# Chunk 0 of an SSM plus SwiGLU kernel: parameters turned by a VectorE block transpose, two evictions split by K tile, activation transposes at other places

## The chip, the cores and the metric

The kernel runs on one core of a Trainium2 chip. The metric is the device time of one execution in microseconds. Every kernel of one round is timed on the same chip, next to runs of the kernel before. A ratio is the mean time of one kernel's fast runs over that of the other's of the same rounds, so it is not quite the ratio of the medians that are quoted. A fast run is within 1.5% of the fastest. One run of the kernel before (181.74 us, in the last round) lies 1.2% above its fastest, far from all others. The ratios of that round include it, and it makes them wide; the ranges, counts and medians quoted below leave it out.

## The reference, cut to what matters

```python
x = A_x                                   # 1 x 2048 x 512, bfloat16
xn = layernorm(x)
# A: diagonal state space model with complex state, 512 states
y = 2 * real(scan(Lam_bar, xn @ B_bar.T) @ C.T) + xn * Dskip
# B: SwiGLU with a hidden size of 1376
f = (silu(xn @ w_gate) * (xn @ w_up)) @ w_down
out = x + y + f
```

`Lam_bar`, `B_bar` and the rotation tables come from three parameter vectors of 512 values each: `Lambda_re`, `Lambda_im`, `log_dt`.

## The kernel before

The 2048 rows are worked in four chunks of 512, each of four tiles of 128 rows. Only chunk 0 matters here. Its tiles are normalised on VectorE and ScalarE, transposed on TensorE (two halves of 256 columns per tile, two 128x128 transposes per half), evicted from PSUM to `xnT` by ScalarE (tiles 0 to 2) or VectorE (tile 3), and multiplied at once with the first 7 column tiles of `w_gate`: 28 matmuls of 128 columns for each tile, called a quarter. Dummy matmuls run before this, to bring TensorE's clock up.

The parameters are loaded as 12 rows of 128 and turned on TensorE, ahead of the last transposes of tile 3:

```python
def pload(name, slot, src, **kw):
    return dma(name, prow[4 * slot:4 * slot + 4, :], src.rearrange("(a p) -> a p", p=128), ...)

def xt_tile_fine(a, h, slot=None):              # tile a, half h
    par = a == 3 and h == 1
    def tr2(e):
        if par:                                                                   # L577
            e.transpose(out=ptr[:, slot, 512:524], in_=prow[:], identity=ident[0:12, 0:12])
        for j in range(2):                                                        # L580
            ... e.transpose(out=ptr[:, slot, j*128:(j+1)*128], in_=xn_sb[...], identity=ident[:])
    ...
    if a == 3:            # VectorE evicts, and copies the parameters out of PSUM (L589)
    elif a == 0 and h == 0:   # ScalarE, one eviction per K tile (L593)
    else:                 # ScalarE, one eviction of 128x256 (L598)
# [cut]
pe_warm(9, 512, wbank); pe_warm(2, 128, wbank)          # dummy matmuls
ln_chunk0()
xt_tile_fine(0, 0, wbank); pe_warm(1, 256, ...); xt_tile_fine(0, 1); pe_warm(1, 256, ...)
for q in range(4):
    for k0, k1 in ((0,1),(1,2),(2,3),(3,4)) if q == 0 else ((0,2),(2,4)):
        for n, (i, bk) in enumerate(tiles):             # 7 column tiles
            if k0 == 0 and n == 1 and q:
                xt_tile_fine(q, 1)
            if k0 == (2 if q else 3) and n == (0, 2, 1, 9)[q]:
                xt_tile_fine(q + 1, 0)
            ... matmul w_gate tile i with xnT of quarter q, K tiles k0 to k1      # L804
```

All transposes of chunk 0 after the first share one PSUM slot, so each must also wait until the previous one is evicted.

## Time and profile before

| | before |
|---|---|
| median of 3 runs | 179.68 us (179.66 to 179.74) |
| span of the profiled execution | 177.8 us |
| TensorE's share of the chain that ended last | 95% |
| quarters of chunk 0, TensorE | 5.93 to 13.42 us |

The page of the kernel before, busy times and the chain by engine:

```profile
PE 173.9 (98%) x936; PEld 83.7 (47%) x936; DVE 163.1 (92%) x284; ACT 88.3 (50%) x114; POOL 9.2 (5%) x21
...
PE 95%; DMA 1%; ACT 1%; DVE 1%; issue 0%
```

TensorE is the chain, and VectorE's 92% is not. From 11.97 us to 175.5 us the chain has no piece but matmuls. So a change that edits none of those matmuls can gain only ahead of 13.42 us. This is the chain there, for the kernel before, in order of time (start us, length us, engine, output and line, count). L804 are the quarters' matmuls, L580 the activation transposes, L577 the parameter transpose, and L760 is the first matmul of 512 columns:

```profile
5.93 1.17 PE pb L804 x21
7.10 0.13 PE pb L580 x2
7.23 0.02 issue
7.25 0.39 ACT xnT L598
7.64 0.05 issue
7.69 0.28 PE pb L804 x2
7.97 0.11 PE pb L580 x2
8.09 0.89 PE pb L804 x16
8.98 0.11 PE pb L580 x2
9.09 0.76 PE pb L804 x12
9.85 0.11 PE pb L580 x2
9.97 0.78 PE pb L804 x14
...
11.64 0.11 PE pb L577
11.75 0.22 PE pb L580 x2
11.97 1.45 PE pb L804 x26
13.42 11.22 PE pb L760 x52
```

How to read it: divide length by count. 14 matmuls in 0.78 us and 26 in 1.45 us are 0.0557 us each; that is TensorE without a wait. 12 in 0.76 us are not: 0.67 would do, so 0.09 us was lost to a wait too short to be a piece of its own. At 7.25 the chain leaves TensorE for an eviction on ScalarE, the one outright wait. The pair after L577 takes 0.22 us where every other takes 0.11 to 0.13.

The timeline of the kernel before shows the same wait at the weight load (PEld), with its releaser; the eviction of tile 2's first half; and the small parameter transpose:

```profile
7.25 0.38 ACT L598 ACTIVATE xnT<-pb 128x256 bf16<-128x256 bf16 x1 [0.85 <-PE pb L580]
7.68 0.11 PEld L804 LDWEIGHTS pb<-xnT,wg 128*128 128x128 bf16 x2 [0.26 <-ACT xnT L598]
...
9.13 0.38 ACT L598 ACTIVATE xnT<-pb 128x256 bf16<-128x256 bf16 x1 [0.62 <-PE pb L580]
...
9.56 0.12 PEld L804 LDWEIGHTS pb<-xnT,wg 128*128 128x128 bf16 x2
...
11.57 0.18 PE L577 MATMUL pb<-ident,prow 12*128 12x12 bf16 x1
```

The timeline of the queue that issues the loads (SP), kernel before: the first parameter load, the load of `w_up` behind the three, and the first of the DMA transposes of B, which waits for all earlier loads:

```profile
3.13 0.37 SPq L401 DMA_DIRECT2D prow<-in_A_log_dt_dram  x1
...
4.18 0.41 SPq L401 DMA_DIRECT2D wu<-in_B_w_up_dram  x1
...
13.72 2.07 SPq L396 DMA_TRANSPOSE BT<-in_A_B_re_dram  x1
```

### The profile page before, as it was taken

Reading aid. Unit: us, or ns where it says so; the run is one execution under the profiler, and the core shown is the slowest. Engines: PE = TensorE matmul, PEld = TensorE weight load, DVE = VectorE, ACT = ScalarE, POOL = GpSimd, SP = SyncE. Lnnn points to the kernel's source line nnn. Section 1 sums busy time; section 2 is a strip of 40 time slices with the busy share of each in tenths; the row PEclk is TensorE's granted clock in tenths of the full one; section 3 lists DMA queues with packets and bytes.
Section 4 is the critical chain, followed back from the end, with each engine's and each line's share of the span. In section 5 each row is a group of like instructions: output and inputs, shape, how many; then the busy total and the mean of one; then the engine's idle time right before and its main releaser. Section 6 shows DMA issues by size and latency. Waiting matters only on the chain.

```text
span 177.8 us, 2427 instructions
## 1 busy us (share of the span) xinstructions
PE 173.9 (98%) x936; PEld 83.7 (47%) x936; DVE 163.1 (92%) x284; ACT 88.3 (50%) x114; POOL 9.2 (5%) x21
## 2 busy tenths in 40 slices
PE   8899999999999999999999999999999999999994
PEld 3794444444444444444444444444444444444743
DVE  2958998997999999999999999999899999999933
ACT  4669989699999674043565660000965520000000
POOL 3023300210000000300000000000000000000000
PEclk9999999999999999999999999999999999999999
DMA  5995563569540000012600000002000000001022
GB/s 162 382 331 118 120 122 118 121 147 329 148 79 0 0 0 0 0 33 85 123 0 0 0 0 4 0 29 81 8 0 4 0 0 0 0 0 49 13 88 89
DMA packets 22978, 12.37 MB, mean 70 GB/s; under 512 B 15192, under 2 KB 22968, under 8 KB 22968
## 3 DMA queue, kind: packets, MB, share of 16 engines
q1 hardware_dynamic: 22472, 11.54, 23.4%
q10 hardware_dynamic: 496, 0.69, 1.2%
q8 instruction: 7, 0.11, 0.3%
q14 instruction: 3, 0.02, 0.0%
HBM read 6.46 MB, written 2.10 MB: 48 GB/s over the span
## 4 chain that ended last, share of the span: by engine, by line
PE 95%; DMA 1%; ACT 1%; DVE 1%; issue 0%
PE pb L760 36%; PE pb L959 21%; PE pb L972 16%; PE pb L876 16%; PE pb L804 3%; PE pb L839 2%; DMA x_sb<-in_A_x_dram 1%; PE pb L849 1%; PE pb L580 1%; DVE st L528 0%; ACT xn_sb L546 0%; ACT xnT L598 0%; ACT sd L522 0%; ACT nm L543 0%; DVE x_sb L977 0%
## 5 line engine op out<-in xcount | busy, mean ns | idle before, releaser
L916 DVE TENSOR_TENSOR_SCAN rot<-sm,car,rot 128x512 bf16<-128x512 f32 x32 | 39.0, 1267 | 0.1
L959 PE MATMUL pb<-wd,hT 128*128 128x512 bf16 (+3 forms) x198 | 38.8, 355 | 0.0
L760 PE MATMUL pb<-xnT,wu 128*128 128x512 bf16 x160 | 37.3, 379 | 0.0
L760 PE MATMUL pb<-xnT,wg 128*128 128x512 bf16 x132 | 31.3, 379 | 0.0
L972 PE MATMUL pb<-W,hss 128*128 128x512 bf16 (+2 forms) x144 | 28.3, 355 | 0.0
L876 PE MATMUL pb<-xnT,BT 128*128 128x512 bf16 x128 | 28.1, 379 | 0.0
L959 PEld LDWEIGHTS pb<-wd,hT 128*128 128x128 bf16 (+1 forms) x198 | 18.5, 98 | 19.9
L772 ACT ACTIVATE sg<-pb 128x1024 bf16<-128x1024 f32 x20 | 20.2, 1025 | 9.4 <-PE pb L760 8.1
L760 PEld LDWEIGHTS pb<-xnT,wu 128*128 128x128 bf16 x160 | 15.6, 98 | 18.9 <-issue 0.2
L829 ACT ACTIVATE uf<-pb 128x1024 bf16<-128x1024 f32 x20 | 20.6, 1028 | 7.5 <-PE pb L760 6.1
L972 PEld LDWEIGHTS pb<-W,hss 128*128 128x128 bf16 x144 | 13.4, 98 | 14.3
L760 PEld LDWEIGHTS pb<-xnT,wg 128*128 128x128 bf16 x132 | 12.7, 98 | 15.7 <-issue 0.8
L876 PEld LDWEIGHTS pb<-xnT,BT 128*128 128x128 bf16 x128 | 12.5, 98 | 15.1
L883 ACT ACTIVATE u_sb<-pb 128x1024 bf16<-128x1024 f32 x16 | 16.3, 1022 | 6.0 <-PE pb L876 5.6
L977 DVE TENSOR_TENSOR x_sb<-pb,x_sb 128x512 bf16<-128x512 f32 (+2 forms) x18 | 11.1, 624 | 3.6 <-PE pb L972 3.4
L831 DVE TENSOR_TENSOR hT<-sg,uf 128x1024 bf16<-128x1024 bf16 x20 | 13.4, 682 | 0.4 <-ACT uf L829 0.4
L504 ACT ACTIVATE xn_sb<-x_sb,nmr,rstd 128x512 bf16<-128x512 bf16 x8 | 6.0, 802 | 9.2 <-DVE nmr L501 9.2
L858 ACT ACTIVATE sg<-pb 96x1024 bf16<-96x1024 f32 x2 | 2.0, 1020 | 17.1 <-PE pb L839 17.1
L907 DVE TENSOR_TENSOR rot<-u_sb,cosT 128x2048 bf16<-128x2048 bf16 x8 | 9.8, 1219 | 0.3 <-ACT u_sb L883 0.3
L907 DVE TENSOR_TENSOR rot<-rot,cosT 128x2048 bf16<-128x2048 bf16 x8 | 9.7, 1218 | 0.1
L907 DVE TENSOR_TENSOR rot<-rot,sin 128x2048 bf16<-128x2048 bf16 x8 | 9.8, 1219 | 0.0
L907 DVE TENSOR_TENSOR rot<-u_sb,sin 128x2048 bf16<-128x2048 bf16 x8 | 9.7, 1218 | 0.0
(82 smaller groups left out, 141.2 us busy)
## 6 DMA issues: line engine op xcount, KB each, us to landing
out_dram<-x_sb SPq DMA_DIRECT2D x15, 128.0 KB, 1.7
x_sb<-in_A_x_dram SPq DMA_DIRECT2D x3, 512.0 KB, 7.1
wd<-in_B_w_down_dram SPq DMA_DIRECT2D x1, 1280.0 KB, 6.4
wu<-in_B_w_up_dram SPq DMA_DIRECT2D x1, 768.0 KB, 5.0
wu<-in_B_w_up_dram SPq DMA_DIRECT2D x1, 608.0 KB, 7.2
x_sb<-in_A_x_dram SPq DMA_DIRECT2D x4, 128.0 KB, 3.5
wg<-in_B_w_gate_dram SPq DMA_DIRECT2D x1, 480.0 KB, 6.0
wg<-in_B_w_gate_dram ACTq DMA_DIRECT2D x1, 448.0 KB, 3.9
```

What stands on the lines that cost most here:

```text
L504: g.add("act", lambda e, a=a: e.activation(out=xn_sb[:, a % NXN, :], in_=x_sb[:, a, :], func=AF.Identity, scale=rstd[:, a:a + 1], bias=nmr ...
L760: inst = e.matmul(pbank[0:fs, bk, :].rearrange("p (j t) -> p j t", j=4), lhsT=w[:, kt, i * 128:i * 128 + fs], rhs=xnT[:, c % 2, :, kt, :], ...
L772: g.add("act", lambda e: e.activation(out=sg[rows, sl, 0:n, :].rearrange("p a t -> p (a t)"), in_=pair_f32(rows, bk, 512 * n), func=AF.Sil ...
L829: g.add("act", lambda e: e.activation(out=uf[rows, ul, 0:n, :].rearrange("p a t -> p (a t)"), in_=pair_f32(rows, bk, 512 * n), func=AF.Ide ...
L831: g.add("dve", lambda e: e.tensor_tensor(out=hT[rows, hb, i0:i0 + n, :], in0=sg[rows, sl, 0:n, :], in1=uf[rows, ul, 0:n, :], op=ALU.mult), ...
L876: inst = e.matmul(pbank[:, bk, :].rearrange("p (j t) -> p j t", j=4), lhsT=BT[:, ri, kt, pt * 128:(pt + 1) * 128], rhs=xnT[:, c % 2, :, kt ...
L883: g.add("act", lambda e: e.activation(out=u_sb[:, us].rearrange("p r t -> p (r t)"), in_=pair_f32(slice(0, 128), b0), func=AF.Identity), r ...
L907: tt = lambda out, a, b, op, r, w, nm: g.add("dve", lambda e: e.tensor_tensor(out=out, in0=a, in1=b, op=op), reads=r, writes=w, name="%s_% ...
L916: g.add("dve", lambda e, A0=A0, A1=A1, k=k, ri=ri, pt=pt: e.tensor_tensor_scan(out=A1[:, k, ri, :], data0=rr[:, pt:pt + 1].to_broadcast([1 ...
L959: inst = e.matmul(pbank[:, bk, 0:nc_], lhsT=hT[0:fs, hb, i, lt * 128:(lt + 1) * 128], rhs=wd[0:fs, i, c0:c0 + nc_], start=(i == 0), stop=F ...
L972: inst = e.matmul(pbank[:, bk, 0:nc_], lhsT=hss[:, hb, pt, ri, lt * 128:(lt + 1) * 128], rhs=W12[:, ri, pt, c0:c0 + nc_], start=False, sto ...
L977: g.add("dve", lambda e, bk=bk, a=a, c0=c0, nc_=nc_: e.tensor_tensor(out=x_sb[:, a, c0:c0 + nc_], in0=pbank[:, bk, 0:nc_], in1=x_sb[:, a, ...
```

## The change

The intent: take the parameter transpose off TensorE, and give each eviction time to end before TensorE needs it. VectorE's transpose is used on 32x32 blocks (the prediction says why), so the rows are loaded in another layout (16 rows of 32 values per vector, spread over 128 partitions), and one VectorE instruction turns them. Tiles 1 and 2 get their first half evicted by K tile, the quarters' matmuls start on the first K tile alone, and the transposes stand a few matmuls earlier or later.

```diff
-        praw = sb("praw", [128, 3, PT], B16)
-        prow = sb("prow", [12, 128], B16)
+        prT = sb("prT", [128, 32], B16)
+        praw = prT[:].rearrange("p (a e) -> p e a", e=8)
+        prow = sb("prow", [128, 32], B16)          # zeroed by GpSimd first
...
-  dma(name, prow[4 * slot:4 * slot + 4, :], src.rearrange("(a p) -> a p", p=128), ...)
+  dma(name, prow[slot:128:8, :], src.rearrange("(a q j) -> q a j", a=4, q=4), ...)
...
-                             ("r", 2, 0), ("n", 2, 0), ("n", 2, 1), ("b", 3, 1), ("s", 3, 0),
+                             ("r", 2, 0), ("n", 2, 0), ("n", 2, 1), ("b", 3, 1), ("s", 3, 0), ("p", 0, 0),
+                elif op == "p":
+                    last = g.add("dve", lambda e: e.transpose(out=prT[:], in_=prow[:]), ...)
...
-                if par:
-                    e.transpose(out=ptr[:, slot, 512:524], in_=prow[:], identity=ident[0:12, 0:12])
-                if par:
-                    g.add("dve", ... tensor_copy(out=praw..., in_=ptr[:, slot, 512:524]) ...)
-            elif a == 0 and h == 0:
+            elif h == 0:
                 for j in range(2):    # one eviction per K tile
...
+            place = {(0, 2, 4): (1, 0), (1, 0, 3): (1, 1), (1, 2, 2): (2, 0), (2, 0, 4): (2, 1), (2, 2, 2): (3, 0), (3, 0, 2): (3, 1)}
             for q in range(4):
-                for k0, k1 in ((0, 1), (1, 2), (2, 3), (3, 4)) if q == 0 else ((0, 2), (2, 4)):
+                for k0, k1 in (((0, 1), (1, 2), (2, 3), (3, 4)), ((0, 1), (1, 2), (2, 4)), ((0, 1), (1, 2), (2, 4)), ((0, 2), (2, 4)))[q]:
                     for n, (i, bk) in enumerate(tiles):
-                        if k0 == 0 and n == 1 and q:
-                            xt_tile_fine(q, 1)
-                        if k0 == (2 if q else 3) and n == (0, 2, 1, 9)[q]:
-                            xt_tile_fine(q + 1, 0)
+                        if (q, k0, n) in place:
+                            xt_tile_fine(*place[(q, k0, n)])
```

Cut: order edges of the scheduler (small parameter operations on VectorE after tile 3's last eviction, on ScalarE after the first silu).

More of the change, by code (lines that the diff above doesn't have):

```diff
@@ L414, in pload @@
         def pload(name, slot, src, **kw):
-            return dma(name, prow[4 * slot:4 * slot + 4, :], src.rearrange("(a p) -> a p", p=128), [("prow", slot)], 1024, **kw)
+            return dma(name, prow[slot:128:8, :], src.rearrange("(a q j) -> q a j", a=4, q=4), [("prow", slot)], 1024, reads=[("prow0",)], **kw)
         def x_load(a, **kw):
@@ L421, in wg_load @@
             return dma("ld_wg" + nm, wg[:, k0:k1, 0:FG], wg_v[:, k0:k1, 0:FG], [("wg", nm)], (k1 - k0) * 128 * FG * 2, **kw)
+        g.add("pool", lambda e: e.memset(prow[:], 0.0), writes=[("prow0",)], name="prow0", est=100)
         x_load(0)
@@ L552, in ln_chunk0 @@
                     last = bn_half(a, h, (last,))
+                elif op == "p":
+                    last = g.add("dve", lambda e: e.transpose(out=prT[:], in_=prow[:]), reads=[("prow", k) for k in range(3)] + [("prow0",)],
+                                 writes=[("praw", k) for k in range(3)], name="parT", est=90, order=(last,))
                 else:
@@ L572, in xt_tile_fine @@
             slot = xt_pair[0] if slot is None else slot
-            par = a == 3 and h == 1
             def tr2(e):
-                if par:
-                    e.transpose(out=ptr[:, slot, 512:524], in_=prow[:], identity=ident[0:12, 0:12])
                 for j in range(2):
@@ L582, in tr2 @@
                 return inst
-            g.add("pe", tr2, reads=[("xh", a, h), ("ident",)] + [("prow", k) for k in range(3) if par], writes=BK(slot), name="xT%d_%d" % (a, h), est=2 * 64 + 100 * par, ninst=2 + par)
+            g.add("pe", tr2, reads=[("xh", a, h), ("ident",)], writes=BK(slot), name="xT%d_%d" % (a, h), est=2 * 64, ninst=2)
             dst, src = xnT[:, 0, a % 4, 2 * h:2 * h + 2, :], ptr[:, slot, 0:256].rearrange("p (k t) -> p k t", k=2)
-            wr = [("xnTh", a, h)] + ([("xnT", 0, a % 4)] if h else [])
+            wr = [("xnTq", a, 2 * h + j) for j in range(2)] + ([("xnT", 0, a % 4)] if h else [])
             if a == 3:
                 t = g.add("dve", lambda e: e.tensor_copy(out=dst, in_=src), reads=BK(slot), writes=wr, name="xTev%d_%d" % (a, h), est=320, order=(hold["xn3"],))
-                if par:
-                    g.add("dve", lambda e: e.tensor_copy(out=praw[:].rearrange("p k a -> p (k a)"), in_=ptr[:, slot, 512:524]),
-                          reads=BK(slot), writes=[("praw", k) for k in range(3)], name="parTev", est=80, order=(t,))
-            elif a == 0 and h == 0:
+            elif h == 0:
                 for j in range(2):
-                    t = g.add("act", lambda e, j=j: e.activation(out=dst[:, j], in_=src[:, j], func=AF.Identity), reads=BK(slot), writes=[("xnTq", j)],
-                              name="xTev0_0%d" % j, est=240, order=(t,) if j else ())
+                    t = g.add("act", lambda e, j=j: e.activation(out=dst[:, j], in_=src[:, j], func=AF.Identity), reads=BK(slot), writes=wr[j:j + 1],
+                              name="xTev%d_0%d" % (a, j), est=240, order=(t,) if j else ())
                     if j == 0:
-                        hold["ev0a"] = t
+                        hold["ev%da" % a] = t
             else:
@@ L626, in small @@
         def small(eng, name, fn, reads, writes, est=90):
-            g.add(eng, fn, reads=reads, writes=writes, name=name, est=est, prio=_CFG['prio_par'], order=(hold["evac"],) if eng == "act" else ())
+            g.add(eng, fn, reads=reads, writes=writes, name=name, est=est, prio=_CFG['prio_par'], order=(hold["evac"],) if eng == "act" else (hold["ev31"],) if eng == "dve" else ())
         def dve_tt(outn, an, bn, op):
@@ L806, in mm @@
                             return inst
-                        g.add("pe", mm, reads=[("wg", "a%d" % max(k - 1, 0)) for k in range(k0, k1)] + ([("xnTq", k0)] if q == 0 and k0 < 2 else [("xnTh", q, k0 // 2)]), writes=BK(bk), name="mm_gq%d_%d_%d" % (i, q, k0),
-                              est=(k1 - k0) * 56, ninst=k1 - k0)
+                        g.add("pe", mm, reads=[("wg", "a%d" % max(k - 1, 0)) for k in range(k0, k1)] + [("xnTq", q, k) for k in range(k0, k1)], writes=BK(bk),
+                              name="mm_gq%d_%d_%d" % (i, q, k0), est=(k1 - k0) * 56, ninst=k1 - k0)
             reserved.clear()
-            seq = ["sd0", "negm0", "nmr0", "xa01", "ev0a", "ev00", "sd1", "ev01", "ev10", "sd2", "ev11", "ev20", "sd3", "ev21"]
+            seq = ["sd0", "negm0", "nmr0", "xa01", "ev0a", "ev00", "sd1", "ev01", "ev1a", "ev10", "sd2", "ev11", "ev2a", "ev20", "sd3", "ev21"]
             for a_, b_ in zip(seq, seq[1:]):
@@ L817, in ffn_gate_quarters @@
                 silu_pair(0, ip, banks[ip])
+            hold["evac"] = [t for t in g.tasks if t.name == "silu0_0"][0]
         def ffn_up(c, ip):
```

## The prediction

> **What bounds the kernel now.** The chain of waits gives TensorE 95% of the 177.8 us span. Its pieces follow one another without a hole from 11.97 us to 175.5 us (L804, L760, L876, L839, L849, L959, L972), at full granted clock. The change edits none of those matmuls, so what can move is the stretch 5.5 to 13.4 us, where chunk 0 is normalised, transposed and multiplied with w_gate in quarters.
>
> That stretch, by the chain of waits: 112 matmuls of 128 columns need 0.0557 us each (x14 takes 0.78, x26 takes 1.45), so 6.24 us; six pairs of activation transposes after the first two need 0.11 each, 0.66. From 5.93 us this would end at 12.83; it ends at 13.42. The excess of 0.59 us:
> - about 0.24 at 7.4 to 7.97 us: the first matmuls of quarter 1 wait for ScalarE's 128x256 eviction (the timeline shows it 7.25 to 7.63; 0.26 us of waiting at the weight load);
> - about 0.09 before the transpose at 9.64, which needs its PSUM slot evicted (ScalarE until 9.51);
> - about 0.22 at 11.64 to 11.97: the 12-row parameter transpose (L577, 0.11) and the pair after it, taking 0.22 where the others take 0.11;
> - 0.02 to 0.04 of rounding.
>
> **What the change does.**
> 1. L577 and the 0.15 us PSUM copy of the parameters (L589) go. A VectorE 32x32 block transpose stands before the last reciprocal, where VectorE idles 0.44 us for ScalarE's square root. The Trainium skill, "VectorE: DVE Perf Modes", section "The three transpose paths", says that VectorE transposes only 32x32 blocks and writes SBUF; hence the new row layout. A 128x32 transpose should cost about 0.15 us, an estimate from the similarly small 0.15 us copy; hidden. It needs the parameter loads by about 9.3 us: issued 3.1 to 4.1, queued ahead of w_up's load, which lands at about 9.2. The loads become 64-byte rows on 16 partitions.
> 2. Two evictions of tiles 1 and 2 are split by K tile. A split pair takes 0.42 us against 0.38, but the first half is there after about 0.22. Quarter 1 then starts without waiting.
> 3. Transposes move: tile 1's first three matmuls earlier, others one to two later, giving the evictions 10 or more matmuls (0.56 us) before use, against about 0.46 from transpose to usable data.
> 4. Parameter arithmetic can begin some 2 us sooner (GpSimd's 1.03 us power starts at 12.64 now), filling VectorE idle time before 13.7 us. This should not move TensorE: ScalarE's first silu (12.90 to 13.92) is done 0.36 us before its bank is needed at about 14.28, and both move together. w_up and w_gate landed before; B's second transpose lands at about 22.0, needed at 24.6.
>
> Laying the new order out with these durations, I get the end of the quarters at about 12.86 instead of 13.42, with slacks of 0.1 to 0.2 us at each eviction. Later, the last state is written by VectorE at 165.7 and read at 168.5, so nothing should take the gain back.
>
> **Predicted:** gain 0.53 us, all on the critical path: 179.15 us, range 178.9 to 179.5. Faster by over 2%: 1%; within 2%: 98%; slower by over 2%: 1%.
>
> **What will show it.** No wait of L804's weight loads for ScalarE; no small transpose on TensorE; the chain reaching its first 512-column matmul at about 12.9 us; an unbroken TensorE chain afterwards; span about 177.3.
>
> **What would make it wrong.** The parameter loads landing after about 9.5 us and holding VectorE ahead of tile 3's normalisation; a slack smaller than computed, so that a tile waits elsewhere; the statically scheduled ScalarE and VectorE orders shifting, so that an early table operation delays a bank release and TensorE stalls after 13 us; or VectorE, 92% busy, pacing a later stage.

## The result, and the profile after

| | before | after |
|---|---|---|
| median of 6 runs | 179.69 us (179.66 to 179.96) | 179.40 us (179.14 to 180.00) |
| ratio of fast runs | | 0.9985 (95%: 0.9968 to 1.0002): the same within 2% |
| profiled execution | 179.60 us, span 177.8 | 179.14 us, span 177.4 |
| first 512-column matmul | 13.42 us | 12.99 us |

The median lies in the predicted range, but three of the six runs (179.54, 179.59 and 180.00) do not, and runs of the changed kernel lie 0.9 us apart where those of the kernel before lay within 0.3. So there are two questions. Why 0.43 us in the profiled execution and not 0.53? And where do the slow executions come from?

The chain of the kernel after (L803 are the quarters' matmuls, L582 the transposes, L759 the first 512-column matmul):

```profile
6.94 0.11 PE pb L582 x2
7.05 0.73 PE pb L803 x13
7.77 0.11 PE pb L582 x2
7.88 0.87 PE pb L803 x15
...
8.87 0.78 PE pb L803 x14
9.65 0.12 PE pb L582 x2
9.77 0.87 PE pb L803 x14
10.64 0.11 PE pb L582 x2
10.75 0.78 PE pb L803 x14
11.54 0.11 PE pb L582 x2
11.65 1.34 PE pb L803 x24
12.99 11.22 PE pb L759 x52
```

The eviction is gone from the chain, and so are L577 and the slow pair behind it. One group is still slow: the 14 matmuls from 9.77 take 0.87 us, where 14 at 8.87 and at 10.75 take 0.78. The timeline of the kernel after, around that place, with VectorE's block transpose (L556) and ScalarE's whole eviction of tile 2's second half (L597):

```profile
9.18 0.20 DVE L556 STREAM_TRANSPOSE prT<-prow 128x32 bf16<-128x32 bf16 x1
...
9.50 0.27 PE L582 MATMUL pb<-ident,xn_sb 128*128 128x128 bf16 x2
...
9.81 0.38 ACT L597 ACTIVATE xnT<-pb 128x256 bf16<-128x256 bf16 x1 [0.21 <-PE pb L582]
```

The block transpose took 0.20 us, waited for nothing, and hid in VectorE's idle time. The eviction ended at 10.19, 0.69 us after the transposes began.

The load queue of the kernel after, as shown for the kernel before:

```profile
3.13 0.71 SPq L402 DMA_DIRECT2D prow<-in_A_log_dt_dram  x1
...
5.04 0.45 SPq L402 DMA_DIRECT2D wu<-in_B_w_up_dram  x1
...
14.71 2.17 SPq L397 DMA_TRANSPOSE BT<-in_A_B_re_dram  x1
```

Here is a cost that the prediction did not count: a parameter load of 16 rows of 64 bytes holds the issuing queue for 0.71, 0.54 and 0.53 us, against 0.37, 0.25 and 0.30 us for 4 rows of 256 bytes. Everything behind starts 0.86 us later, and B's transposes 1.0 us later.

### The profile page after: what moved, and what is told of

Read it like the earlier page. It is cut to its first block, busy times and chain, and to the rows that moved or that the text cites. A ratio compares the mean times of both kernels' runs of the same rounds, so it can differ in the third digit from the quotient of the medians.

```text
span 177.4 us, 2421 instructions
## 1 busy us (share of the span) xinstructions
PE 173.6 (98%) x927; PEld 83.8 (47%) x935; DVE 162.5 (92%) x284; ACT 88.1 (50%) x116; POOL 9.0 (5%) x22
## 4 chain that ended last, share of the span: by engine, by line
PE 95%; DMA 1%; DVE 1%; ACT 1%; issue 0%
PE pb L759 36%; PE pb L959 21%; PE pb L876 16%; PE pb L972 15%; PE pb L803 4%; PE pb L839 2%; DMA x_sb<-in_A_x_dram 1%; PE pb L849 1%; PE pb L582 1%; DVE st L530 0%; ACT xn_sb L548 0%; ACT nm L545 0%; ACT sd L524 0%; DVE x_sb L977 0%; DVE mv L522 0%
## 5 line engine op out<-in xcount | busy, mean ns | idle before, releaser
L959 PE MATMUL pb<-wd,hT 128*128 128x512 bf16 (+3 forms) x194 | 38.1, 355 | 0.2
L759 PE MATMUL pb<-xnT,wu 128*128 128x512 bf16 x160 | 37.3, 379 | 0.0
L759 PE MATMUL pb<-xnT,wg 128*128 128x512 bf16 x132 | 31.3, 379 | 0.0
L759 PEld LDWEIGHTS pb<-xnT,wu 128*128 128x128 bf16 x160 | 15.6, 98 | 18.9 <-issue 0.2
L759 PEld LDWEIGHTS pb<-xnT,wg 128*128 128x128 bf16 x132 | 12.7, 98 | 15.7 <-issue 0.4
L482 DVE BATCH_NORM_STATS2 st<-x_sb 128x6 f32<-128x512 bf16 x12 | 7.4, 678 | 2.9 <-DMA x_sb<-in_A_x_dram 2.9
```

The source lines that it names most:

```text
L482: return g.add("dve", lambda e, a=a: e.bn_stats(out=st[:, a, :], in_=x_sb[:, a, :]), reads=[("x", a)], writes=[("st", a)], name="bnst%d" % ...
L759: inst = e.matmul(pbank[0:fs, bk, :].rearrange("p (j t) -> p j t", j=4), lhsT=w[:, kt, i * 128:i * 128 + fs], rhs=xnT[:, c % 2, :, kt, :], ...
L959: inst = e.matmul(pbank[:, bk, 0:nc_], lhsT=hT[0:fs, hb, i, lt * 128:(lt + 1) * 128], rhs=wd[0:fs, i, c0:c0 + nc_], start=(i == 0), stop=F ...
```

## The experiments

Three theories of the slow executions were on the table first. L: the late load queue sometimes starves TensorE. T: the new transpose places are too tight. V: VectorE's block transpose sometimes waits for its rows. After the first four runs, C joined: TensorE's clock comes up late in some executions.

### The changed kernel again

No edit.

> The changed kernel again, unedited, to see whether its spread (179.14 to 180.0 us in six runs, where before gives 179.66 to 179.96) is its own. If it is a property of the kernel, its runs again spread over 0.4 us or more while before stays within 0.3; fastest about 179.15, mean about 179.4, ratio about 0.9985. If the spread was an accident, all runs lie within 0.2 us, near 179.2.

Measured: 179.14, 179.21, 179.23, 179.37, 179.74 us, beside nine runs of the kernel before at 179.60 to 179.87 us; ratio 0.9980 (0.9967 to 0.9992). In this round the changed kernel spreads over 0.60 us and the kernel before over 0.27, as if the spread were the change's own. The later rounds don't bear that out: there the kernel before spreads over 0.46 and 0.45 us too. The profiled execution again had the 0.87 us group, and all pieces from tile 1's first transposes on, to 0.01 us.

### Parameters on TensorE, the rest of the change kept

```diff
-   prow [128, 32], 16-row loads, VectorE block transpose before the last reciprocal
+   prow [12, 128], 4-row loads, e.transpose(prow) on TensorE before tile 3's second half, PSUM copy
```

> New places and split evictions, but the parameters loaded in 12 rows and turned on TensorE as before. Theory L (the 16-row parameter loads hold up the load queue, and what is loaded behind them arrives late in some runs): no spread, about 179.35 us (the 0.24 and 0.09 us of waiting gone, the 0.2 us of the parameter transpose still there), w_up issued at about 4.2 us, the chunk 1 rows landed by 13.8. Theory T (the new transpose places have too little slack, and a tile waits in some runs): the same spread as the full change, up to 180. Theory V (VectorE's block transpose waits for its rows in some runs and holds tile 3): no spread either.

Measured: 179.44, 179.47, 179.57, 179.58, 179.97 us; ratio 0.9994 (0.9982 to 1.0007). The load queue was as predicted by L (`w_up` issued at 4.17 us), yet one run of five lay 0.5 us above the fastest. Neither "no spread" (L, V) nor "the same spread" is clear from five runs. The chain again shows 0.11 us for the parameter transpose and 0.22 us for the pair after it.

### Parameters on VectorE, places and evictions as before

```diff
-   place = {...}; three K steps in quarters 1 and 2; split evictions of tiles 1 and 2
+   the places, two K steps and whole evictions of the kernel before
```

> Places and evictions as before, parameters by 16-row loads and VectorE block transpose. Theories L and V: the spread appears here, runs from about 179.45 to 180.3. Theory T: no spread, about 179.45 us (0.2 us of parameter transpose gone, the waits still there).

Measured: 179.74, 179.77, 179.82, 180.06, 180.11 us; ratio 1.0011 (0.9998 to 1.0023). No run showed the gain, although the chain of the profiled execution shows that it is there, with no parameter transpose and the last pair at 0.11 us:

```profile
12.01 0.11 PE pb L582 x2
12.12 1.45 PE pb L803 x26
13.57 11.22 PE pb L759 x52
```

So the stretch was shorter, but it began later: its first transposes of tile 1 ended at 7.60 us and not at 7.23. Its dummy matmuls of 256 columns took 0.42 us, against 0.27 in the kernel before and the changed one: TensorE ran at about half speed until past 6 us. That turned the question from the stretch to what comes ahead of it, and is where theory C comes from. The Trainium skill, "TensorE: Matmul & The Clock Gate", section "Part 1: The HAM clock gate (the "warmup" mystery)", says that the array starts at half speed and is released by a busy, free-running window, so that the release falls at another time in each run. Here the trace agrees: the weight loads of the quarters' matmuls come 0.107 us apart up to about 6.3 us, and 0.056 us apart after it.

### Parameter rows loaded last

```diff
-   three parameter loads ahead of w_up's load; block transpose before tile 3's reciprocal
+   three parameter loads behind the load of chunk 1's rows; block transpose among chunk 1's statistics
```

> The full change, but the three parameter loads are issued after the chunk 1 rows, and the block transpose stands among chunk 1's statistics, after tile 3 is normalised. Theory L: bulk loads are issued as early as in before (w_up about 3.1 us), B's transposes at about 13.7 and 17.8 us, no spread, 179.15 to 179.25 us. Theory V: no spread too, since nothing of chunk 0 waits for the rows any more. Theory T: spread as in the full change.

Measured: 179.31, 179.39, 179.50, 179.54, 180.08 us; ratio 0.9985 (0.9971 to 0.9999). This fits no theory as it stood: nothing of chunk 0 waits for the parameter rows any more, the bulk loads are issued early, and the spread is still there. In the profiled execution (180.08 us) the chain began with a load of `w_gate`:

```profile
1.71 5.60 DMA wg<-in_B_w_gate_dram
```

The same load took 4.2 to 4.4 us in the two executions of the changed kernel profiled so far. Here the load of `w_up`, issued at 3.12 and not at 5.04 us, was in flight beside it. That the early bulk loads slow it down is suggested by this one look; no run isolates it. The clock of this execution was late too (6.1 us, and 0.42 us for the dummies of 256 columns), but the chain goes back to the load.

### Three more loads that nobody reads

```diff
+   for slot, src in ((2, A_log_dt), (1, A_Lambda_im), (0, A_Lambda_re)):
+       dma(..., pdum[slot:128:8, :], src.rearrange("(a q j) -> q a j", a=4, q=4), ...)   # kernel before, behind its own loads
```

> The kernel before, plus three 16-row loads of the parameters into a tile that nobody reads, issued behind the 12-row loads. Theory L (the 16-row loads' cost on the load queue lengthens or scatters the time): w_up issued about 1.7 us later than the 4.2 us of before, B's first transpose at about 15.5 instead of 13.7 us, and runs of 179.8 to 180.2 us. Theory C (the slow runs are those in which TensorE's clock comes up late, after about 5.3 us; the load queue has slack enough): 179.7 us as before, although the loads are late.

Measured: 179.64, 179.66, 179.80, 179.88, 179.89 us; ratio 0.9996 (0.9984 to 1.0009), against nine runs of the kernel before at 179.67 to 180.13 us. The load queue of this kernel:

```profile
6.03 0.45 SPq L402 DMA_DIRECT2D wu<-in_B_w_up_dram  x1
...
16.75 2.10 SPq L397 DMA_TRANSPOSE BT<-in_A_B_re_dram  x1
```

B's first transpose starts 3 us later than in the kernel before, 2 us later than in the changed one, and TensorE's chain does not notice. Theory L falls: the queue's delay is real, and costs nothing that the ratio (to about 0.2 us) or the chain (to 0.03 us, by the table below) can show.

### Two tiny matmuls at the end of the changed kernel

```diff
         dc_chunk(3, split_last=True)
+        pe_warm(2, 32, 0)
```

> The changed kernel with two 32-column matmuls added at TensorE's very end, off every path. If the spread of the changed kernel comes with the mere length or placing of TensorE's program, its runs move as a group against those of the changed kernel (179.14 to 180.0). If it is chance from run to run, the same spread, fastest 179.15, mean about 179.4. In its profile, theory C expects the time above 179.14 to be half of what the last cold matmul lies past 5.2 us.

Measured: 179.19, 179.19, 179.34, 179.50, 179.73 us; ratio 0.9976 (0.9960 to 0.9991). The same kind of spread, and no shift as a group; so nothing points to the program's length. The profiled execution (179.34 us) corrects theory C: its clock was up early, at 3.9 us (the start of the trace's clock record), and it still lost 0.20 us, because the first rows of x landed later (that piece of the chain is 2.41 us long, against 2.25) and all that follows from them was late. So C alone does not cover the spread.

### Whole evictions, the new places kept

```diff
-            elif h == 0:            # tiles 0, 1, 2: one eviction per K tile
+            elif a == 0 and h == 0: # tile 0 alone
```

> The full change with the evictions of tiles 1 and 2 left whole; TensorE's order as in the change. By the laid-out timeline the eviction of tile 1's first half ends at about 7.47 us, ready by about 7.52, and TensorE reaches quarter 1 at about 7.6: no wait, so the same time as the full change within 0.1 us (fastest 179.15): the earlier place does it and the split is a reserve. If the split is what removes the wait, about 0.1 to 0.2 us slower and a wait of the weight load for ScalarE at 7.5 us.

Measured: 179.44, 179.44, 179.82, 179.82, 179.89 us; ratio 0.9991 (0.9978 to 1.0005). The expectation was wrong: the split is no reserve. Two groups in the chain became slower, 13 matmuls from 0.73 to 0.82 us and 14 from 0.78 to 0.87:

```profile
7.54 0.82 PE pb L803 x13
...
9.46 0.87 PE pb L803 x14
```

### The kernel before, a second profile

> The kernel before, unedited, for a second profile: theory C expects a run near 179.68 us to have a clock that is up by about 5.3 us (3.8 in the first profile).

Measured: 179.58 us, clock up at 5.0 us. As theory C expected, but a clock at 5.0 us is also consistent with no effect at all; it only bounds where the effect begins.

### All evictions of tiles 1 and 2 split

```diff
-            elif h == 0:
+            elif h == 0 or a:        # tiles 1 and 2: second halves too
-   quarters 1 and 2: K steps (0,1), (1,2), (2,4)
+   quarters 1 and 2: K steps (0,1), (1,2), (2,3), (3,4)
```

> The full change, and the second-half evictions of tiles 1 and 2 split too, with quarters 1 and 2 multiplied in four K steps. In the change's trace TensorE still loses 0.09 us where quarter 2's second half waits for the whole eviction (the 14 matmuls after 9.65 us take 0.87 where others take 0.78), and about 0.03 us in quarter 1. If that reading is right, both are gone: those 14 take 0.78, the first 512-column matmul stands 0.10 to 0.13 us earlier relative to the first transposes than in the change, and the fastest runs are at 179.02 to 179.06 us. If the loss is of another kind (ScalarE's order, VectorE), they still take 0.87 and the time is 179.14.

Measured: 179.21, 179.22, 179.28, 179.48, 179.66, 179.66 us; the changed kernel in the same rounds 179.30 to 179.70. The group that took 0.87 us takes 0.78 now:

```profile
10.26 0.12 PE pb L582 x2
10.37 0.78 PE pb L803 x14
```

The reading of the trace was right, and the 15 matmuls of quarter 1 went from 0.87 to 0.84 us. But tile 1's second pair of transposes now took 0.17 us and not 0.11, so 0.07 us is left of the 0.12. The means of six runs are 179.42 and 179.44 us: the times cannot tell the two kernels apart, and the fastest run missed the expected 179.06. The same 0.06 us also appeared in two other kernels (parameters on TensorE, rows last), so it seems to be a tight place, where the shared slot comes free just in time, and not a cost of this edit; no run tests that.

The profiled execution (179.66 us) had a late clock. The dummy matmul of 256 columns shows it. The page's clock row is no help: this execution has none (its trace has no clock record), and that of the changed kernel shows full speed in all 40 slices, the first ones included. So a late clock has to be read from durations. First the timeline of this kernel, then that of the changed one (L477 are the dummies):

```profile
5.30 0.42 PE L477 MATMUL pb<-const-bfloat16-1.0 128*128 128x256 bf16 x1
```

```profile
5.06 0.27 PE L477 MATMUL pb<-const-bfloat16-1.0 128*128 128x256 bf16 x1
```

### The changed kernel, a third time

> The changed kernel, unedited, beside the others on the same chip. Theory C (TensorE's clock comes up at a time that differs from run to run, between about 3.5 and 7 us, and what comes after about 5.3 us delays everything) expects a mix again: most runs at 179.14 to 179.25, some up to 180.0.

Measured: 179.30, 179.35, 179.36, 179.45, 179.46, 179.70 us; ratio 0.9964 (0.9934 to 0.9995), to eleven runs of the kernel before, the one of 181.74 us among them; without it the means give 0.9975. A mix, with none at 179.14 to 179.25, where most were expected. The profiled execution (179.70 us) had an early clock and another cause: VectorE's statistics waited for a load of x, tile 1 was normalised 0.57 us late, and the weight load of its first transposes waited for that:

```profile
6.39 0.43 DVE L512 BATCH_NORM_STATS2 st<-x_sb 128x6 f32<-128x256 bf16 x1 [0.56 <-DMA x_sb<-in_A_x_dram]
...
7.31 0.11 PEld L582 LDWEIGHTS pb<-ident,xn_sb 128*128 128x128 bf16 x2 [0.40 <-DVE xn_sb L517]
```

### The dummy matmuls begun later, in both kernels

```diff
-            pe_warm(9, 512, wbank)
+            pe_warm(6, 512, wbank, reads=[("car", 0, 0)])   # begins after a GpSimd memset at about 2.1 us
```

> The changed kernel with TensorE's dummy matmuls begun at about 2.2 us instead of 0.83 and three fewer, so that they still end before the first transposes at about 5 us. Theory C: the clock comes up about 1.4 us later, between about 4.9 and 8.3 us, so nearly all runs are late ones: 179.3 to 180.6 us, mean about 179.8, and the profile shows the 256-column dummy matmuls at 0.42 us and matmuls of 128 columns spaced at about 0.107 us past 6 us. If the slow runs of the change come from loads or from VectorE instead, nothing changes: 179.14 to 180.0, most at 179.2.

> The same later and shorter dummy matmuls in the kernel before. Theory C: it suffers as the changed kernel does, 179.8 to 181.1 us, mean about 180.3, some 0.5 us above the late-started change. If the old order had waits that absorb a late clock, it stays at 179.7 to 179.9.

Measured: the kernel before went to 179.68, 180.15, 180.23, 180.26, 180.32, 180.76 us (its unedited runs beside it: 179.67 to 180.12), ratio 1.0009 (0.9976 to 1.0042) with the run of 181.74 us among the unedited ones and 1.0019 without it, and its profiled execution shows the 256-column dummies at 0.42 us. The changed kernel went to 179.21, 179.28, 179.39, 179.51, 179.74, 180.34 us, hardly more than unedited (179.30 to 179.70); its profiled execution (179.28 us) happened to have the clock up at 5.1 us. So the runs of the kernel before came out where theory C expected them, though by the ratio the shift is not clear of noise, and those of the changed kernel only partly: their mean is 179.58 us and not 179.8. That a late clock costs time is seen in the profiled executions that had one. How many of six runs start late is a matter of luck.

## Why the prediction was right or wrong

**All executions at once.** The spread can be taken out. Let T be the end of tile 1's first pair of transposes in the chain, and M the start of the first 512-column matmul. M minus T is the stretch that the change works on; the rest of the time lies ahead of T or behind M. Every profiled execution, from its chain:

| kernel | T | M | M - T | time | time - T |
|---|---|---|---|---|---|
| before | 7.23 | 13.42 | 6.19 | 179.60 | 172.37 |
| before, second profile | 7.23 | 13.43 | 6.20 | 179.58 | 172.35 |
| before, extra loads | 7.27 | 13.46 | 6.19 | 179.66 | 172.39 |
| before, late dummies | 7.89 | 14.08 | 6.19 | 180.23 | 172.34 |
| parameters on VectorE only | 7.60 | 13.57 | 5.97 | 179.74 | 172.14 |
| parameters on TensorE | 7.20 | 13.42 | 6.22 | 179.57 | 172.37 |
| whole evictions | 7.54 | 13.66 | 6.12 | 179.82 | 172.28 |
| changed kernel | 7.05 | 12.99 | 5.94 | 179.14 | 172.09 |
| changed, again | 7.03 | 12.97 | 5.94 | 179.14 | 172.11 |
| changed, third | 7.60 | 13.54 | 5.94 | 179.70 | 172.10 |
| changed, tail matmuls | 7.22 | 13.16 | 5.94 | 179.34 | 172.12 |
| changed, late dummies | 7.16 | 13.10 | 5.94 | 179.28 | 172.12 |
| changed, rows last | 7.94 | 13.94 | 6.00 | 180.08 | 172.14 |
| all split | 7.63 | 13.50 | 5.87 | 179.66 | 172.03 |

The five executions of the changed kernel's stretch, from 179.14 to 179.70 us, agree within 0.03 us in time minus T. So do those of the kernel before, within 0.05. All but these few hundredths of the spread of the profiled executions lies ahead of T, and it has several causes, each seen in a trace: a late clock, late rows of x, a late `w_gate`. Of these, the unedited changed kernel showed only late rows of x, in its third profile.

The change has a part in that one. It puts tile 1's first transposes three matmuls earlier. In the five executions of the changed kernel's stretch their first weight load starts 0.05 us after VectorE has normalised that half tile (6.69 and 6.75 us in the first profile), which means at once. In the three profiles of the old order with the dummies as they were and no late clock (before, second profile, extra loads) it starts 0.17, 0.09 and 0.19 us after. So the new place has no slack left for late rows of x: in the third profile the weight load waits 0.40 us there, and at the old place it would have waited about 0.23 (an estimate, 3 x 0.0557 us less). Theory T was right in this part. No experiment moves this one place alone.

The old order has 91 quarter matmuls between T and M, the new one 94 (tile 1's transposes stand three earlier), so the old 6.19 us compare as 6.19 + 3 x 0.0557 = 6.36. From T on, the change is worth 6.36 - 5.94 = 0.42 us, with an early clock or a late one; where tile 1's rows come late, up to 0.17 us of it are given back ahead of T, by the estimate above. Over all runs of all rounds, which were not all on one chip, the medians are 179.73 us for the kernel before (34 runs) and 179.36 us for the changed one (17 runs).

**Point by point.**

1. *TensorE bounds the kernel, and only 5.5 to 13.4 us can move.* Right. After 12.99 us the chain is the old one, shifted; the last VectorE addition starts 0.43 us earlier (175.53 to 175.10).
2. *0.22 us for the parameter transpose and the pair after it.* Right: with the parameters alone on VectorE, M - T falls by 0.22 us. Why the pair behind L577 took twice as long was not tested further.
3. *The block transpose costs about 0.15 us and hides.* 0.20 us measured, and hidden. The Trainium skill, "VectorE: DVE Perf Modes", section "The three transpose paths", gives 311 ns for 128x128 in 32x32 blocks; a quarter of the columns took 0.20 us, well over a quarter of that time.
4. *Quarter 1 starts without waiting; 0.24 us.* The wait is gone, and the new place and the split each took a part of it. In the old order 7 matmuls stand between tile 1's first transposes and quarter 1, in the new one 10. With the old place the weight load waited 0.26 us; with the new places and whole evictions 0.09 us were lost (13 matmuls in 0.82 us and not 0.73); with the split, nothing. Yet over the whole stretch the places alone gain only 0.02 us: M - T is 6.12 with whole evictions, against 5.97 + 0.17 = 6.14 with the old places. They took from others what they gave quarter 1: tile 2's second half has 10 matmuls behind it where it had 12, and now loses 0.09 us; tile 1's second half has 11 where it had 12, and loses 0.03. The split gains 0.18 us on top, 0.09 each for the first halves of tiles 1 and 2. The split at the old places was not run.
5. *"Giving the evictions 10 or more matmuls (0.56 us) before use, against about 0.46 from transpose to usable data", with slacks of 0.1 to 0.2 us.* This is the step that failed. The 0.46 us was counted from the end of the transposes; the 10 matmuls must be counted from their start, since TensorE issues them right behind (0.11 us after the transposes' start, by the timeline of after: 9.50 and 9.61). From the start of tile 2's transposes (9.50) to the end of the eviction (10.19) is 0.69 us, and 0.05 us more until TensorE sees it, as the issue piece of before shows. The pair and 10 matmuls cover 0.11 + 0.56 = 0.67 us. The slack is -0.07 us, and 0.09 us were lost. The same sum holds for the whole evictions: every pair with 10 matmuls behind it and a whole eviction on ScalarE lost 0.09 us (three groups), the one with 11 lost 0.03, and the loss vanished where that eviction was split. The 0.09 and the 0.03 us make up the 0.11 us between the predicted 0.53 and the 0.42 us. The trace of the kernel before already held the counterexample. The prediction put the 0.09 us ahead of 9.64 down to a transpose that waits for its PSUM slot; the gap lies at quarter 2's first weight load (9.56), the transposes follow it without one, and the pair that it waited for had 10 matmuls behind it.
6. *The loads, the tables and the later stages take nothing back.* Right in the outcome. The parameters' power on GpSimd starts 3.2 us sooner (9.47 us, 12.64 before) and nothing on TensorE's chain shows it. The prediction missed that the 16-row loads hold the queue 0.86 us longer; extra loads showed that more than twice that delay is free.
7. *The range.* The median of 179.40 us is inside. The prediction says nothing of a spread from run to run; the three runs of the kernel before that were known then lay within 0.08 us. Over all 17 runs of the changed kernel, 5 lie above 179.5, so the range held single runs about 7 times in 10. The median gain in the first six runs, 0.29 us, is about half of the 0.53 us predicted; that it still fell into the range owes to the range's width.

**What stays open.** Which of the three causes acted in the runs without a profile is unknown. Whether the changed kernel is late more often is unsettled: 7 of its 17 runs lie over 0.25 us above its fastest, and 11 of 34 of the kernel before. The lost slack ahead of T speaks for it, but no run tests that.

## What to carry to other kernels

When one engine feeds another through an eviction, count the slack from the issue of the producer and not from its end, because the consumer's own queue goes on in the meantime. Moving an instruction passes slack from one wait to another: here it took 0.17 us off one eviction's wait, brought back 0.12 at two others, and used up what slack the transposes had ahead of them. Splitting an eviction so that its first piece is usable early gained 0.18 us, and at most 0.06 of it was lost again in single executions, perhaps because the two pieces hold the slot longer (0.45 us against 0.38). When an effect is a quarter of a percent and runs differ by more, find a point in the chain that the change cannot move, and compare traces from there on: five traces agreed within 0.03 us where their times spread over 0.56. A cost on a queue (0.86 us of load issue here) is no cost of the kernel until a trace shows who waits for it.

## What the Trainium skill lacked or had wrong

- "TensorE: Matmul & The Clock Gate", section "Part 1: The HAM clock gate (the "warmup" mystery)", says that the clock rises after a busy window of about 3.4 us, that the window is free-running, and that the transition varies by about 500 ns from run to run. A free-running window fits: where the trace's clock record of full speed exists, in nine executions, it is 174.08 us long each time, 51 times 3.413 us, wherever it starts. The 500 ns are too few: with dummies that begin at 0.83 us, the record starts anywhere from 3.5 to 6.1 us (a later note of the same section, 6 to 14 cold matmuls in one kernel, fits better). And a whole busy window was not needed: 3.47 us is 2.64 us after the first dummy that the profile shows.
- No page says how the time for which a load holds its issuing queue depends on its rows: 4 rows of 256 bytes 0.25 to 0.37 us, 16 rows of 64 bytes 0.53 to 0.71 us, for the same 1 KB (and 2.14 us once, behind the bulk loads, in the kernel with the rows last). "DMA: Bandwidth & Descriptors", section "Anatomy of one DMA — SWDGE (gpsimd) path", calls descriptor generation small and variable, but for DMAs that GpSimd issues, and these are issued by SP.
- "VectorE: DVE Perf Modes", section "The three transpose paths", has a time for 128x128 alone: 311 ns. A 128x32 block transpose took 0.20 us here.
